# Second layer of a two-layer MoE block: the first product by Strassen's seven block products

## The chip, the cores and the metric

One core of a Trainium2 chip runs the whole program. The engines are named as in the profile: PE is TensorE (PEld are its weight loads), DVE is VectorE, ACT is ScalarE, POOL is GpSimd, and SP is SyncE, whose queue issues nearly all DMAs. The metric is the device time of one execution in microseconds (us). Before the change it is 1785.63 us, the median of 3 runs (1784.83 to 1786.25).

## The reference

Pooled attention (batch 8, 8 heads, 576 tokens, head size 64, keys and values averaged over 8 positions) gives `x` of 4608 x 512. Two feed-forward layers follow, each with d_ff = 2048:

```python
def _moe_ref(x, w_in, w_out):          # layer 1
    h = np.maximum(x @ w_in, 0.0)
    return (h * h @ w_out).astype(np.float32)

def _moe2_ref(x, w_in, w_out):         # layer 2
    h = x @ w_in
    g = np.maximum(0.01 * h, h)
    return (g @ w_out).astype(np.float32)
```

The weights come as float64. Every product of float32 numbers is computed as three products of parts of type `float32r`: a number is split into a high part and the remainder, its low part, and high x high, low x high and high x low are added up. For layer 2 this is 3 x 2 x 4608 x 512 x 2048 multiply-adds.

## The kernel before

The tokens are handled in 9 blocks of 512 (`T = 512`, `BLOCKS = 9`), d_ff in 16 chunks of 128 (`FC = 16`), d_model in 4 pieces of 128 (`KC = 4`). `run(blk)` is called for blocks 2 to 17: numbers up to 8 are layer 1, numbers 9 to 17 are layer 2 (`ph` is 0 or 1). Blocks 0 and 1 of layer 1 are done earlier by `first_products` and `second_products`, mixed with attention.

Within `block`, chunk by chunk, `first` makes `h` for one chunk: 12 matmuls (4 pieces of the contraction times 3 part products) of 128 x 128 weights by 512 tokens into one PSUM bank out of four (`ps`). `between` takes that bank off (ACT), applies the activation function and splits the result into `gh` and `gl` (DVE). `second` multiplies it by the chunk of `w_out`: 12 matmuls of 512 columns into the four banks `acc0` to `acc3`, which collect over all 16 chunks. The products are staggered: `first` of chunk u+1 stands ahead of `second` of chunk u, so that `between` has a whole `second` and the next `first` to hide behind. `finish` copies the four banks out and stores them.

All of this is written out by hand (`tc.manual_schedule()`): each engine executes its instructions in the order in which the program calls them. A wait therefore holds up everything behind it on the same engine. SBUF tiles come from one pool, with a number of buffers for each tag; a tile waits until the last use of the buffer's earlier tile is over.

The weights of layer 2 are converted from float64 during layer 1: `Stored.tick` does one of six steps for half of a weight pair at a time and stores high and low parts to DRAM (`w2_parts`). During block 8, the last of layer 1, `fetch` loads them into the buffers that layer 1's weights leave free.

The lines that the prediction speaks of are L860 (matmuls of `first`), L906 (matmuls of `second`), L888 and L889 (activation of layer 2), L878 and L879 (splitting), L343 and L344 (splitting layer 2's weights), L672 and L673 (splitting `x`, where the ACT copies and the DVE subtracts) and L695 to L698 (attention's values, whose matmuls have many widths).

## Time and profile before

| what | value |
|---|---|
| median of 3 runs | 1785.63 us (1784.83 to 1786.25) |
| span of the profiled execution | 1783.2 us; the profile gives no other time for it, and the median is 2.4 us above the span |
| PE busy | 1735.8 us, 97% of the span |
| DVE busy | 944.9 us, 53% |
| ACT busy | 510.8 us, 29% |
| chain that ended last | PE 91%, DVE 6%, ACT 2% |
| block 8 (last of layer 1) | 908.2 to 995.3 us |
| layer 2 (blocks 9 to 17) | 995.3 to 1778.6 us, 3456 matmuls |

The page has one row for each engine with its busy time, and the chain of work that ended last, which is followed back from the last instruction. Since matmuls overlap, a matmul's own duration is longer than the distance between two of them: read the distance from start to start.

### The profile page before, as it was taken

What the parts mean: (1) busy time and instruction counts of PE and PEld (TensorE: products, weight loads), DVE (VectorE), ACT (ScalarE), POOL (GpSimd) and SP (SyncE); (2) the same over time, 40 slices, a digit from 0 to 9 for tenths busy, and PEclk for the clock granted to TensorE, in tenths of its full rate; (3) what the DMA queues carried; (4) which work ended last, traced back from release to release, by engine and by line L of the source; (5) the groups of instructions that cost most, each with busy time, mean ns of one, the idle gap of its engine ahead of it and who ended that gap; (6) DMA issues with size and microseconds to landing.
All of it is one profiled execution on the core that took longest, in us unless ns stands there. A gap on an engine that the chain in (4) does not pass through costs nothing.

```text
span 1783.2 us, 20649 instructions
## 1 busy us (share of the span) xinstructions
PE 1735.8 (97%) x8024; PEld 1437.4 (81%) x8024; DVE 944.9 (53%) x1701; ACT 510.8 (29%) x1269; POOL 18.9 (1%) x37
## 2 busy tenths in 40 slices
PE   6889999999999999999999999999999999999998
PEld 5768778888788888878888888888888888888887
DVE  7888777667666776774322334343434343333333
ACT  4545333343443434433432211111111111111111
POOL 0011000000000000000000000000000000000000
PEclk9999999999999999999999999999999999999999
DMA  8914542332233232222035301010101010101000
GB/s 231 338 65 155 172 158 99 103 107 94 84 107 106 95 120 92 87 80 77 1 135 199 139 1 47 1 48 1 47 1 47 1 48 0 48 7 42 18 7 24
DMA packets 95585, 144.01 MB, mean 81 GB/s; under 512 B 42624, under 2 KB 42752, under 8 KB 93440
## 3 DMA queue, kind: packets, MB, share of 16 engines
q1 hardware_dynamic: 92928, 134.31, 22.9%
q0 software_dynamic: 2560, 8.39, 1.2%
q8 instruction: 63, 1.03, 0.2%
q14 instruction: 34, 0.28, 0.0%
HBM read 98.64 MB, written 44.04 MB: 80 GB/s over the span
## 4 chain that ended last, share of the span: by engine, by line
PE 91%; DVE 6%; ACT 2%; issue 1%; DMA 0%; SPq 0%; DVEq 0%; ACTq 0%
PE acc L906 42%; PE ps L860 39%; PE acc L860 4%; PE ps L581 2%; PE ps L644 1%; PE ps L545 1%; PE acc L375 1%; DVE xl L673 0%; DMA wi<-in_moe_w_in 0%; PE ps L696 0%; ACT s L602 0%; PE ps L698 0%; PE ps L697 0%; PE ps L695 0%; PE ps L650 0%
## 5 line engine op out<-in xcount | busy, mean ns | idle before, releaser
L860 PE MATMUL ps<-xh,wi 128*128 128x512 f32 x2048 | 673.5, 391 | 0.0
L860 PEld LDWEIGHTS ps<-xh,wi 128*128 128x128 f32 x2048 | 384.5, 188 | 79.9 <-issue 0.2
L860 PE MATMUL ps<-xl,wi 128*128 128x512 f32 x1024 | 398.5, 389 | 0.0
L889 DVE SCALAR_TENSOR_TENSOR r<-r 128x512 f32<-128x512 f32 x144 | 99.7, 693 | 462.3 <-ACT r L888 462.3
L906 PE MATMUL acc<-gh,wo 128*128 128x512 f32 x1152 | 297.3, 396 | 4.0 <-DVE gh L878 1.9
L906 PE MATMUL acc<-wo,gh 128*128 128x512 f32 x1152 | 288.9, 389 | 0.0
L888 ACT COPY r<-ps 128x512 f32<-128x512 f32 x144 | 84.5, 587 | 655.6 <-PE ps L860 655.6
L906 PEld LDWEIGHTS acc<-gh,wo 128*128 128x128 f32 x1152 | 214.0, 189 | 50.8 <-DVE gh L878 4.0
L906 PEld LDWEIGHTS acc<-wo,gh 128*128 128x128 f32 x1152 | 216.2, 188 | 44.9
L878 DVE CAST gh<-r 128x512 fp32r<-128x512 f32 x256 | 109.2, 426 | 227.4 <-ACT r L873 213.6
L860 PEld LDWEIGHTS ps<-xl,wi 128*128 128x128 f32 x1024 | 192.3, 188 | 38.9
L879 DVE TENSOR_TENSOR gl<-r,gh 128x512 fp32r<-128x512 f32 x256 | 177.4, 693 | 21.5 <-DVE gh L878 0.5
L906 PE MATMUL acc<-gl,wo 128*128 128x512 f32 x576 | 160.2, 393 | 0.0
L906 PE MATMUL acc<-wo,gl 128*128 128x512 f32 x576 | 158.3, 389 | 0.0
L870 ACT ACTIVATE r<-ps 128x512 f32<-128x512 f32 x112 | 67.7, 605 | 234.2 <-PE ps L860 234.2
L906 PEld LDWEIGHTS acc<-gl,wo 128*128 128x128 f32 x576 | 109.0, 189 | 23.5
L906 PEld LDWEIGHTS acc<-wo,gl 128*128 128x128 f32 x576 | 108.1, 188 | 22.5
L602 ACT ACTIVATE s<-ps,m 128x72 f32<-128x72 f32 x240 | 72.1, 329 | 106.2 <-DVE m L593 106.1
L873 ACT ACTIVATE r<-r 128x512 f32<-128x512 f32 x112 | 70.8, 632 | 3.6
L860 PE MATMUL acc<-xh,wi 128*128 128x512 f32 x128 | 44.4, 413 | 8.7 <-DVE wi L287 5.0
L602 ACT ACTIVATION_READ_ACCUMULATOR s<-ps,m 128x1 f32 x224 | 48.1, 215 | 0.0
L550 ACT COPY qt<-ps 128x512 f32<-128x512 f32 x32 | 18.8, 587 | 87.4 <-PE ps L545 87.4
(150 smaller groups left out, 1365.9 us busy)
## 6 DMA issues: line engine op xcount, KB each, us to landing
w2p<-val SPq DMA_DIRECT2D x32, 512.0 KB
pth<-x SPq DMA_DIRECT2D x9, 1024.0 KB
wi<-in_moe_w_in SPq DMA_DIRECT2D x8, 1024.0 KB
wo<-in_moe_w_out SPq DMA_DIRECT2D x8, 1024.0 KB
val<-in_moe_w_in SPq DMA_DIRECT2D x16, 512.0 KB
val<-in_moe_w_out SPq DMA_DIRECT2D x16, 512.0 KB
wi<-w2p SPq DMA_DIRECT2D x8, 1024.0 KB
wo<-w2p SPq DMA_DIRECT2D x8, 1024.0 KB
```

What stands on the lines that cost most here:

```text
L375: nc.tensor.matmul(ps[:n, c * 2 * D : (c + 1) * 2 * D], lhsT=ident[:n, :n], rhs=raw[:n, r * 2 * D : (r + 1) * 2 * D], start=r == 0, stop=r ...
L550: nc.scalar.copy(qT[i].rearrange("p c t -> p (c t)"), ps)
L581: nc.tensor.matmul(ps[: r0 + n, c2 * PAIR : (c2 + 1) * PAIR], lhsT=qt[:, cc, : r0 + n], rhs=kts[b][:, keys], start=True, stop=True,)
L602: nc.scalar.activation(out=s[:, g, :], in_=ps[:, h * SP : (h + 1) * SP], func=AF.Exp, bias=m[:, g : g + 1], accum_out=None if i in early e ...
L860: nc.tensor.matmul(ps, lhsT=w[:, kc], rhs=x[kc], start=(kc == 0 and n == 0), stop=(kc == KC - 1 and n == 2),)
L870: nc.scalar.activation(out=r, in_=ps, func=AF.Relu)
L873: nc.scalar.activation(out=r, in_=r, func=AF.Square)
L878: nc.vector.tensor_copy(gh, r)
L879: nc.vector.tensor_tensor(out=gl, in0=r, in1=f32(gh), op=ALU.subtract)
L888: nc.scalar.copy(r, ps)
L889: nc.vector.scalar_tensor_tensor(out=r, in0=r, scalar=0.01, in1=r, op0=ALU.mult, op1=ALU.max)
L906: nc.tensor.matmul(acc[m], lhsT=w[:, piece] if ph == 0 else x[:, piece], rhs=x if ph == 0 else w, start=(c == 0 and n == 0), stop=(c == FC ...
```

## The change

Layer 2's first product is no longer computed chunk by chunk over 512 tokens. Tokens come in 6 spans of 768, each made of two halves of 384 (`TS`). A group is one span with a pair of chunks of d_ff. The contraction (512) is cut in two halves of 256, so that the product of a group is a 2 x 2 block product, and Strassen's method (in Winograd's form) computes it with 7 block products of 256 x 128 x 384 in place of 8. Every block product takes 6 matmuls of 384 columns (2 pieces of the contraction times 3 part products). The sums of blocks that the seven products need are made ahead: of `x` by `x_sum`, `x_high`, `x_low` (tiles `fh0` to `fh6`, `fl0` to `fl6`), of the weights by `make_in`. The sums behind the products are made partly in PSUM, where products 2, 3, 5 and 6 add to what stands in their bank, and partly by DVE (`use`).

The seven forms of weights take more room, so only 8 of the 16 chunks are in SBUF at a time: one pass over all spans with the first 8 chunks, whose results are stored to DRAM (`part`), then one pass back over the spans with the other 8, to whose results `part` is added. The spans' order in the second pass is reversed, so that the span at the turn stays loaded. The second product is as before 36 matmuls of 512 columns for a group; `piece(g - 1, j)` puts six of them behind each of the first six block products of the next group. Two banks alternate for the block products, six collect results.

Of layer 2's weights, `w_in` is stored in float32 (`w2_raw`, out of a tile `r`) and no longer split in layer 1; `w_out` as before. In block 8, `early` loads and splits the first span and makes the first weights. The names in SBUF are spread over several pools, so that buffers can be given over to layer 2.

```diff
@@ Stored.tick @@
-            elif k == 4:
+            elif k == 4 and h % 2:
                 t = sb([P, 2, 512], F32R, "val")
-                nc.vector.tensor_copy(t[:, 0, :], f32(self.val))
+                nc.vector.tensor_copy(t[:, 0, :], self.out)
...
+            elif k == 5 - (h + 1) % 2:
+                i, n = h // 4, h // 2 % 2
+                to = w2_parts[i, :, :, n * 512 : (n + 1) * 512] if h % 2 else w2_raw[i, :, n]
+                nc.sync.dma_start(out=to, in_=self.out)
@@ second layer @@
+    FORMS = (A11, S2, A12, S3, S1, A22, S4)
...
+            self.order = [(0, n) for n in range(SPANS)] + [(1, n) for n in reversed(range(SPANS))]
+            self.groups = [(*o, p) for o in self.order for p in range(PAIRS)]
...
+        def x_high(self, j):
+            nc.scalar.copy(self.xh[j], self.x_raw(j))
+        def x_low(self, j):
+            nc.vector.tensor_tensor(
+                out=self.xl[j], in0=self.x_raw(j), in1=f32(self.xh[j]), op=ALU.subtract
+            )
...
+        def product(self, g, j):
+            half, n, p = self.groups[g]
+            at = self.banks[(g + j) % 2][:, :TS]
+            hi, lo = self.weights[p]
+            m = 0
+            for w, x in ((hi, self.xh), (lo, self.xh), (hi, self.xl)):
+                for kc in range(2):
+                    nc.tensor.matmul(
+                        at,
+                        lhsT=w[:, FORMS[j], kc],
+                        rhs=x[j][:, kc],
+                        start=m == 0 and j in (0, 1, 4),
+                        stop=m == 5,
+                        skip_group_check=True,
+                    )
+                    m += 1
+            self.use(g % 2, j, at)
+        def use(self, k, j, at):
+            def add(out_, x):
+                nc.vector.tensor_tensor(out=out_, in0=x, in1=at, op=ALU.add)
+            if j == 0:
+                self.s1 = sb([P, TS], F32, "gh")
+                nc.scalar.copy(self.s1, at)
+            elif j == 1:
+                self.u2 = sb([P, TS], F32, "gl")
+                add(self.u2, self.s1)
+                self.flush()
+            elif j == 2:
+                self.h11 = sb([P, TS], F32, "h11")
+                nc.scalar.copy(self.h11, at)
+            elif j == 3:
+                self.u3 = sb([P, TS], F32, "u3")
+                add(self.u3, self.s1)
+                self.leaky(self.h11, k, 0, 0)
+            elif j == 4:
+                add(self.u3, self.u3)
+                self.leaky(self.u3, k, 1, 1)
+            elif j == 5:
+                add(self.s1, self.s1)
+                self.leaky(self.s1, k, 1, 0)
+            else:
+                add(self.u2, self.u2)
+                self.flush()
+                self.leaky(self.u2, k, 0, 1)
+        def leaky(self, h, k, c, t):
+            nc.vector.scalar_tensor_tensor(
+                out=h, in0=h, scalar=0.01, in1=h, op0=ALU.mult, op1=ALU.max
+            )
+            hi, lo = self.gh[k][c][t], self.gl[k][c][t]
+            nc.scalar.copy(hi, h)
+            self.flush()
+            self.late.append(
+                lambda: nc.vector.tensor_tensor(out=lo, in0=h, in1=f32(hi), op=ALU.subtract)
+            )
...
+        def piece(self, g, i):
+            half, n, p = self.groups[g]
+            t, at = i // (TT // 2), slice(i % (TT // 2) * P, (i % (TT // 2) + 1) * P)
+            order = [(self.gh, c, m) for c in range(2) for m in range(2)]
+            order += [(self.gl, c, 0) for c in range(2)]
+            for m, (x, c, part_) in enumerate(order):
+                nc.tensor.matmul(
+                    self.acc[i],
+                    lhsT=x[g % 2][c][t][:, at],
+                    rhs=self.outs[p][:, part_, c],
+                    start=p == 0 and m == 0,
+                    stop=p == PAIRS - 1 and m == 5,
+                )
+            if p < PAIRS - 1:
+                return
+            if half == 0:
+                st, to = self.result_tile(i), part
+                nc.scalar.copy(st, self.acc[i])
+            else:
+                st, to = self.begun.pop(i), out
+                nc.vector.tensor_tensor(out=st, in0=st, in1=self.acc[i], op=ALU.add)
+            nc.sync.dma_start(out=to[self.rows(n, i), :], in_=st)
+        def group(self, g):
...
+            for j in range(7):
+                self.product(g, j)
+                if after != n and p == 2 and j in (1, 2, 4):
+                    self.x_sum((1, 2, 4).index(j))
+                if after != n and p == 3:
+                    if j >= 2:
+                        self.x_low(j - 2)
+                    if j == 4:
+                        self.x_sum(3)
+                    self.x_high(j)
+                if before != n and p == 0 and j < 2:
+                    self.x_low(5 + j)
+                if g and j < 6:
+                    self.piece(g - 1, j)
...
```

`after != n` holds in the groups of a span behind which another span follows, `before != n` in those behind such a change of span; there are 10 of these changes (five in each pass). `p` is the pair of chunks, 0 to 3.

On PE, layer 2's steady part read before: the end of one `first` (weights `wi`), then a `second` (weights `wo`), then the next `first`.

```order
L860 MATMUL ps<-xl,wi_7750 128x512
L860 MATMUL ps<-xh,wi_7750 128x512
L906 MATMUL acc_8276<-wo_7796,gh 128x512 x2
L906 MATMUL acc_8277<-wo_7796,gh 128x512 x2
L906 MATMUL acc_8278<-wo_7796,gh 128x512 x2
L906 MATMUL acc_8279<-wo_7796,gh 128x512 x2
L906 MATMUL acc_8276<-wo_7796,gl 128x512
```

Now, in the second group (`ps_8339` and `ps_8340` are the two alternating banks, `fh`, `fl` the forms of `x`, `sh`, `sl` the split activations of the group before):

```order
L1345 MATMUL acc0_8333<-wo0_7773,sh_8317 128x512 x2
L1345 MATMUL acc0_8333<-wo0_7773,sh_8319 128x512 x2
L1345 MATMUL acc0_8333<-wo0_7773,sl_8325 128x512
L1345 MATMUL acc0_8333<-wo0_7773,sl_8327 128x512
L1278 MATMUL ps_8339<-fh_7696,wi2_8103 128x384 x2
L1278 MATMUL ps_8339<-fh_7696,wi3_8104 128x384 x2
L1278 MATMUL ps_8339<-fl_7703,wi2_8103 128x384 x2
L1345 MATMUL acc1_8334<-wo0_7773,sh_8317 128x512 x2
```

Twelve matmuls of 512 columns with one bank became six of 384, and each of them is followed by only six of 512 before the next; the last two of a piece need the low parts `sl`.

On DVE, where one block of layer 2 met the next, a chunk was three instructions (activation, high part, low part), then came the split of the next block's `x` (L673), two results (L921) and the next chunk:

```order
L889 SCALAR_TENSOR_TENSOR r<-r 128x512
L878 CAST gh<-r 128x512
L879 TENSOR_TENSOR gl<-r,gh 128x512
L673 TENSOR_TENSOR xl<-pth,xh 128x512 x4
L921 COPY raw<-acc_8277 128x512
L921 COPY raw<-acc_8279 128x512
```

Now, in the fourth group of the first span, behind products 4, 5 and 6, when the next span's forms are being made (L1291 adds a product, L1319 is the activation, L1326 a low part, L1188 a low part of `x`, L1178 a sum of `x`):

```order
L1291 TENSOR_TENSOR u3_8669<-u3_8669,ps_8340 128x384
L1319 SCALAR_TENSOR_TENSOR u3_8669<-u3_8669 128x384
L1326 TENSOR_TENSOR sl_8329<-h11_8653,sh_8321 128x384
L1188 TENSOR_TENSOR fl_7704<-xl_8407,fh_7697 128x768
L1178 TENSOR_TENSOR xl_8407<-xl_8407,t2_8549 128x2x384
L1291 TENSOR_TENSOR gh_8622<-gh_8622,ps_8339 128x384
L1319 SCALAR_TENSOR_TENSOR gh_8622<-gh_8622 128x384
L1326 TENSOR_TENSOR sl_8332<-u3_8669,sh_8324 128x384
L1188 TENSOR_TENSOR fl_7705<-xh_8405,fh_7698 128x768
L1291 TENSOR_TENSOR gl_8637<-gl_8637,ps_8340 128x384
L1326 TENSOR_TENSOR sl_8331<-gh_8622,sh_8323 128x384
```

The work on the next span's `x` now stands in the same queue as the sums and low parts of the products; the last row is the low part that the next group's piece 0 takes in its sixth matmul.

## Rows read from the trace of the kernel before

**Rows 1.** The page: span, busy time of each engine, the chain by engine.
```profile
span 1783.2 us, 20649 instructions
PE 1735.8 (97%) x8024; PEld 1437.4 (81%) x8024; DVE 944.9 (53%) x1701; ACT 510.8 (29%) x1269; POOL 18.9 (1%) x37
PE 91%; DVE 6%; ACT 2%; issue 1%; DMA 0%; SPq 0%; DVEq 0%; ACTq 0%
```
**Rows 2.** Busy time by windows: blocks of layer 1, block 8, layer 2.
```profile
core 0: us, PE busy (x) PEld busy (x) DVE busy (x) ACT busy (x) POOL busy (x), PEclk, DMA share, GB/s
624.00:880.00 256.00, 251.90 (x1206) 209.47 (x1205) 159.49 (x320) 100.30 (x299) 0.00 (x0) 0.99 0.25 80
908.20:995.30 87.10, 87.10 (x386) 72.12 (x385) 21.53 (x38) 22.93 (x38) 0.00 (x0) 1.00 0.56 206
995.30:1778.60 783.30, 783.30 (x3456) 648.27 (x3454) 291.27 (x483) 111.74 (x194) 0.00 (x0) 1.00 0.07 25
```
**Rows 3.** Timeline of a chunk of layer 2: start, duration, engine, line, tiles.
```profile
1103.67 0.39 PE L860 MATMUL ps<-xh,wi 128*128 128x512 f32 x1
...
1103.90 1.98 PE L906 MATMUL acc<-wo,gh 128*128 128x512 f32 x8
1104.10 0.59 ACT L888 COPY r<-ps 128x512 f32<-128x512 f32 x1 [4.85 <-PE ps L860]
1104.72 0.69 DVE L889 SCALAR_TENSOR_TENSOR r<-r 128x512 f32<-128x512 f32 x1 [3.42 <-ACT r L888]
...
1105.51 0.43 DVE L878 CAST gh<-r 128x512 fp32r<-128x512 f32 x1
```
**Rows 4.** Timeline of PE where attention's values have 384 columns (16 matmuls).
```profile
275.97 0.33 PE L695 MATMUL ps<-pth,v_hi 128*128 128x384 f32 x1
276.14 0.34 PE L696 MATMUL ps<-pth,v_lo 128*128 128x384 f32 x1
...
278.60 0.34 PE L698 MATMUL ps<-ptr,v_rem 96*128 96x384 f32 x1
278.77 0.63 PE L906 MATMUL acc<-gh,wo 128*128 128x512 f32 x2
```
**Rows 5.** The chain in time near the start: start, time, engine, tile, line.
```profile
29.89 5.37 PE acc L375 x48
```
**Rows 6.** Groups by line and form: weight loads, and L375's matmuls.
```profile
L906 PEld LDWEIGHTS acc<-wo,gh 128*128 128x128 f32 x1152 | 216.2, 188 | 44.9
L375 PE MATMUL acc<-wo,cst 128*128 128x128 f32 x32 | 3.8, 278 | 0.0
```
**Rows 7.** Groups by line and form on DVE: count, busy us, mean ns, idle before.
```profile
L673 DVE TENSOR_TENSOR xl<-ps,xh 128x384 fp32r<-128x384 f32 x8 | 4.2, 554 | 1.6 <-ACT xh L672 1.1
L879 DVE TENSOR_TENSOR gl<-r,gh 128x512 fp32r<-128x512 f32 x256 | 177.4, 693 | 21.5 <-DVE gh L878 0.5
L287 DVE TENSOR_TENSOR wi<-val,wi 128x1024 fp32r<-128x1024 f32 x8 | 9.7, 1219 | 0.0
L889 DVE SCALAR_TENSOR_TENSOR r<-r 128x512 f32<-128x512 f32 x144 | 99.7, 693 | 462.3 <-ACT r L888 462.3
L921 DVE COPY raw<-acc 128x512 f32<-128x512 f32 x20 | 12.9, 684 | 2.1 <-PE acc L906 2.1
L343 DVE CAST val<-r 128x512 fp32r<-128x512 f32 x32 | 13.6, 425 | 0.9
L344 DVE TENSOR_TENSOR val<-r,val 128x512 fp32r<-128x512 f32 x32 | 22.2, 693 | 1.1
```
**Rows 8.** Groups by line and form on ACT.
```profile
L672 ACT CAST xh<-ps 128x384 fp32r<-128x384 f32 x8 | 3.8, 478 | 3.8 <-PE ps L698 3.7
L672 ACT CAST xh<-pth 128x512 fp32r<-128x512 f32 x36 | 19.6, 620 | 0.0
L283 ACT CAST wi<-val 128x1024 fp32r<-128x1024 f32 x8 | 8.5, 1062 | 4.8 <-DVE val L280 4.8
```
**Rows 9.** Timeline of the end of the program.
```profile
1778.23 0.39 PE L906 MATMUL acc<-wo,gl 128*128 128x512 f32 x1
1779.38 0.33 SPq L924 DMA_DIRECT2D out<-raw  x1
```

More of the change, by code (lines that the diff above doesn't have):

```diff
@@ L86, in attention_relu2_leaky_kernel @@
     BUFS.update({"m": 4, "l": 4, "st": 3, "val": 2})
+    POOLS = {tag: weights for i in range(FC // 2) for tag in (f"wi{i}", f"wo{i}")}
+    POOLS.update({f"wo{i}": spare for i in range(FC // 4, FC // 2)})
+    POOLS.update({tag: common for tag in "cst raw r gh gl st xh xl".split()})
     def sb(shape, dt, tag):
+        pool = POOLS.get(tag, attn)
         return pool.tile(shape, dt, tag=tag, name=tag, bufs=BUFS.get(tag, 1))
@@ L100, in attention_relu2_leaky_kernel @@
     x2 = dram.tile([DM, NT], F32, tag="x2", name="x2")
-    w2_parts = dram.tile([2, FC // 2, P, 2, 1024], F32, tag="w2p", name="w2p")
+    w2_raw = dram.tile([FC // 2, P, 2, 512], F32, tag="w2r", name="w2r")
+    w2_parts = dram.tile([FC // 2, P, 2, 1024], F32, tag="w2p", name="w2p")
+    part = dram.tile([NT, DM], F32, tag="part", name="part")
     mid = dram.tile([2, FC, P, T], F32, tag="mid", name="mid")
@@ L357, in finish @@
                 self.tick()
-        def fetch(self, kind, i):
-            t = sb([P, 2, 1024], F32R, weight_tag(kind, i))
-            nc.sync.dma_start(out=f32(t), in_=w2_parts[kind, i])
-            place(kind, i, t)
     first_tiles, first_s, early = range(T // P), [], range(2 * T // P)
@@ L880, in in_parts, with between, second @@
         return gh, gl
-    def between(ph, blk, ps):
+    def between(blk, ps):
         r = sb([P, T], F32, "r")
-        if ph == 0:
-            relu(r, ps)
-            square(r)
-        else:
-            nc.scalar.copy(r, ps)
-            nc.vector.scalar_tensor_tensor(
-                out=r, in0=r, scalar=0.01, in1=r, op0=ALU.mult, op1=ALU.max
-            )
+        relu(r, ps)
+        square(r)
         return in_parts(r)
-    def second(ph, c, acc, g):
+    def second(c, acc, g):
         gh, gl = g
         wh, wl = woh[c], wol[c]
-        ms = range(KC if ph == 0 else T // P)
+        ms = range(KC)
         passes = (wh, gh), (wl, gh), (wh, gl)
@@ L912, in second, with finish @@
             )
-    def finish(ph, t0, acc):
-        tags = ("st", "raw" if ph or t0 + T == NT else "r")
-        to = x2[:, t0 : t0 + T] if ph == 0 else out[t0 : t0 + T, :]
-        for m in range(KC if ph == 0 else T // P):
-            st = sb([P, T if ph == 0 else DM], F32, tags[m % 2])
+    def finish(t0, acc):
+        tags = ("st", "raw" if t0 + T == NT else "r")
+        for m in range(KC):
+            st = sb([P, T], F32, tags[m % 2])
             if m % 2:
@@ L954, in slot @@
                 done += 1
-        g = between(ph, blk, first(blk, 0))
+        g = between(blk, first(blk, 0))
         chunk_done("in", 0)
@@ L968, in block @@
                     turn.pop(0)()
-            second(ph, u, acc, g)
+            second(u, acc, g)
             chunk_done("out", u)
@@ L973, in block @@
             g = g_next
-        finish(ph, t0, acc)
+        finish(t0, acc)
     w1, w2 = Weights(w1_in, w1_out), Stored(w2_in, w2_out)
@@ L1101, in second_products @@
                 turn.pop(0)()
-            second(0, c, acc, g)
+            second(c, acc, g)
             if 4 <= u < 9:
@@ L1128, in chunk_done @@
+        steps, turn = [], []
+        if not last:
+            steps, turn = all_steps[blk + 1], value_steps(blk + 1, (blk + 1) * T)
         def chunk_done(what, c):
-            if blk < BLOCKS - 1:
+            if last:
+                layer2.early(what, c)
+            else:
                 w2.tick()
-            if blk == BLOCKS - 1:
-                w2.finish()
-                if c % 2 and (what == "in" or c < FC - 1):
-                    w2.fetch(what == "out", c // 2)
-        block(ph, blk, i * T, steps, turn, chunk_done)
@@ L1150, in attention_relu2_leaky_kernel @@
         second_products()
-        for blk in range(2, 2 * BLOCKS):
+        for blk in range(2, BLOCKS):
             run(blk)
+        layer2.run()
 _INS = ["q", "k", "v", "moe_w_in", "moe_w_out", "moe2_w_in", "moe2_w_out"]
```

229 lines of the change are left out of this document (187 added, 42 removed).

## The prediction

> **What bounds the kernel now.** I read the page first: PE is busy 97% of the span of 1783.2 us, and the chain that ended last is 91% PE [rows 1]. An average hides stages, so the busy time by windows comes next. In layer 2, from 995.3 to 1778.6 us, PE is busy for all of the 783.3 us, with 3456 matmuls, a granted clock of 1.00 (the upper level, 2.4 GHz), DVE at 291 us and ACT at 112 us [rows 2]. So layer 2 is a stream of matmuls without a gap, 783.3 / 3456 = 0.2267 us apart. The timeline of one chunk shows why: ACT takes a product off while PE already does 12 matmuls of another kind, and the activations come long before they are wanted [rows 3]. DVE waits 462 us for ACT's copies there [rows 7]. Only fewer or shorter matmuls can shorten this stage, as long as the others keep up.
>
> **The matmuls.** The second product keeps its 1728 matmuls of 512 columns: 48 groups of 36, before 9 blocks of 192. The first had 9 x 192 = 1728 of 512 columns and gets 48 x 42 = 2016 of 384 columns. What one of 384 takes, attention's values show: 16 of them start from 275.97 to 278.60 us and the next instruction at 278.77, that is 2.80 / 16 = 0.175 us each [rows 4]. The difference to 0.2267 is 0.052 us for 128 columns, 2.5 columns a nanosecond; so a matmul costs its columns at the upper clock and about 13 ns. I take 0.174, since one in four of those has 96 rows. First products: before 1728 x 0.2267 = 391.7, after 2016 x 0.174 = 350.8 us. **Gain 40.9 us.** Bounds of the distance: 0.173 (0.2267 less 128 columns at 2.4 GHz), and from above the weight load, below.
>
> The Trainium skill, "TensorE: Matmul & The Clock Gate", section "Back-to-back issue gap", gives for streams of weight load and matmul 81 ns at 128 columns and 131 ns at 512. On a straight line between them, 384 columns would take 114 ns, 0.87 of 512 columns, an estimate from that page. The rows differ, with 0.77 for 384 against 512 and 227 ns where the page has 131, so I count by the rows. By the page's ratio the change would lose, which is a rival below.
>
> **What must keep up.** In a group PE now needs 42 x 0.174 + 36 x 0.2267 = 15.5 us. DVE has 13 instructions of 384 columns: 5 additions out of PSUM, 4 activations, 4 low parts. The nearest row has 0.554 us for 384 columns out of PSUM [rows 7], together 7.2 us. ACT has 6 copies, at 0.478 for 384 columns out of PSUM [rows 8], about 3 us. Both are half idle or more, so the throughput holds. What decides is the order in the queues, with only two banks for block products and with low parts that the pieces read.
>
> In an undisturbed group it holds: from the end of a product to the next use of its bank lie two pieces and a product (1.36 + 1.04 + 1.36 = 3.8 us), or a product and a piece (2.4 us) behind products 5 and 6, and DVE has at most three instructions, 1.7 us, for each.
>
> At the 10 changes of span it doesn't quite. In the fourth group DVE also makes low parts and a sum of the next `x`, of 768 columns: 0.96 us each, halfway between 0.693 for 512 and 1.219 for 1024 [rows 7]. Follow the queue from where product 4 can be read, with DVE idle there, to the low part that piece 0 of the next group takes in its sixth matmul: 8 instructions of 384 and 3 of 768 columns, 8 x 0.554 + 3 x 0.956 = 7.3 us. Add 0.25 for the hand-overs from DVE to DVE, some 0.1 us each: an activation ends at 1105.41 and the next starts at 1105.51 [rows 3]. That is 7.55 us. On PE the same stretch is piece, product 5, piece, product 6, product 0, five matmuls: 2 x 1.36 + 3 x 1.04 + 1.13 = 6.97 us, of which 0.2 are gone before product 4 can be read (ACT starts 0.43 us after a product's last matmul started [rows 3], against a distance of 0.17 to 0.23). So PE waits 7.55 - 6.77 = 0.8 us, with the hand-over **0.9 us, 10 times: 9 us lost**. The bounds: nothing, if DVE's instructions overlap a little (0.08 us each would do), and 2 us a change, if each takes 10% longer and the delay also reaches product 2, which adds into the bank that ACT empties late. I stay with 9, since all durations are rows of this shape or next to it.
>
> **The start of layer 2.** Group 0 has no pieces to put between: 7.3 us of PE against 7.2 us of DVE in a chain, behind two copies of `finish` at 0.68 [rows 7]: 2 us lost (0 to 4), the last group's short wait for its low parts included. The end stays: the last result still passes one DVE instruction (0.69 by its 512 columns, as L921) and one store, 5 us from the last matmul to the end of the span [rows 9, 1]; `part` is loaded a span ahead.
>
> **Layer 1.** Block 8 gets DVE work: 11 instructions on `x` of 0.96 us, and four times about 4 us (four sums of 256 columns, low parts of 256, 512 and 1024) for the weights, together 27 us. ACT gets 7 casts of 0.83 (between 0.620 for 512 and 1.062 for 1024 [rows 8]) and four times 2 us, 14 us. DVE and ACT are busy 21.5 and 22.9 us of 87.1 there [rows 2], and the largest lump, 4 us, meets a slack of 2 x 5.44 us less two chunks' own 1.1: free. If it weren't, each lump would cost at most its 4 us. The loads of 1.6 MB have 13 us, at 206 GB/s and more [rows 2] they take 8. In blocks 2 to 7 DVE loses 16 times 0.43 + 0.69 us [rows 7], 18 us off an engine that has slack; PE is idle there only 4 us of 256 [rows 2], so that can give 1 or 2 us. Against that, 16 stores now leave from a tile `r` out of three, and an activation two chunks later waits for the store. I count 0 (from -2 to +5).
>
> **Sum.** 1783.2 - 40.9 + 9 + 2 = 1753.3 us of span. The runs' median is 1785.6, 2.4 above the span; with that 1755.7, said as **1755.5 us**, with its own range 1748 to 1764.
>
> **The rivals.**
> - No wait at the changes of span and none at the start: 1785.6 - 42 = 1744. For it: 0.9 us is a small difference of two sums of 7 us. Against it: nothing in the rows makes DVE faster. 12%.
> - The delay isn't made good: DVE and ACT stand late through the next span's first two groups too, where low parts 5 and 6 of `x` and six copies or additions of results (0.69 each) follow. Some 2 us more a change, 1755.5 + 20 = 1775. For it: both queues are in strict order. Against it: the third group's slack is 8 us. 13%.
> - Layer 1 waits for the stores out of `r`: 16 x 0.5 = 8, 1764. For it: three buffers. Against it: nearly 3 us of slack by the chunk's 5.44. 8%.
> - Slower: the weight load sets the pace of short matmuls. One load takes 188 ns in the trace [rows 6], longer than the 174 that I count; if loads came one behind the other with 13 ns between, a matmul of 384 would take 201 ns, 2016 x 0.027 = 54 us more, 1810. It decides from 0.189 us (40.9 - 11 = 30 us over 2016). For it: four in five of PE's time in layer 2 has a load running [rows 2]. Against it: 48 matmuls took 5.37 us early on, 0.112 us each [rows 5], of 128 columns and with a weight load each (as many as matmuls, 8024 [rows 1]), so loads do overlap; a row of that line shows its form [rows 6]. 4%.
> - Time falls less than columns do, 0.87 of the distance: 0.198 us, 2016 x 0.024 = 48 us more, 1804. For it: nothing in this trace. Against it: 16 in a row at 0.175 [rows 4]. 3%. The page named above has the rule behind it.
>
> **How the numbers follow.** My forecast has 60%, the rivals 12, 13, 8, 4 and 3%. The range 1744 to 1775 takes in the forecast, the third rival and about half of the first two. A difference of 0.2% (3.6 us) is what runs of this kernel can tell. Slower are the last two rivals, 7%; within it perhaps a mixture of the middle ones, 3%; faster the rest, 90%.
>
> **What would show it.** Right: 2016 matmuls of 384 columns 0.17 to 0.18 us apart; 10 waits of PE of about 1 us in the first group of a span, at the matmul that takes a low part, with DVE as the releaser; DVE busy some 50% of layer 2; layer 2 about 753 us long. Wrong: a distance near 0.19 or more, waits for a bank in every group, block 8 longer than 88 us, or a granted clock below 1.00 in layer 2.

## The result and the profile after

The changed kernel took **1761.6 us** (median of 4 runs, 1759.83 to 1763.66) against 1785.23 us (4 runs, 1783.91 to 1786.25) of the kernel before in the same job: a ratio of **0.9868, 95% interval 0.9854 to 0.9881**. It is faster by 1.3%. The forecast was 1755.5 us, its range 1744 to 1775; the time lies in the range, 6 us above the forecast, and two errors of opposite sign stand behind that, as will be seen.

Line numbers below are the changed kernel's: L864 and L903 are layer 1's two products (L860 and L906 before), L1278 the block products of 384 columns, L1345 the pieces of the second product of 512 columns, L1291, L1319, L1326, L1188 and L1178 VectorE's additions, activations, low halves of the values, low halves of `x` and sums of `x`, L1185 and L1323 ScalarE's high halves, L1295 its copies of products.

The page of the profile first: span, busy times, the chain.

```profile
span 1758.0 us, 21696 instructions
PE 1715.1 (98%) x8312; PEld 1463.6 (83%) x8312; DVE 1112.0 (63%) x2020; ACT 627.8 (36%) x1496; POOL 18.9 (1%) x37
PE 88%; DVE 7%; ACT 2%; DMA 1%; issue 1%; SPq 0%; DVEq 0%; ACTq 0%
```

Against [rows 1], PE has 288 matmuls more and 20.7 us less to do, DVE 167 us more, and the chain is still PE's. The profiled execution itself took 1759.83 us. The busy time by windows comes next: the middle of layer 1, the stretch in which the kernel before did block 8, and layer 2.

```profile
624.00:880.00 256.00, 252.37 (x1193) 206.18 (x1192) 154.00 (x310) 100.41 (x299) 0.00 (x0) 1.00 0.24 75
908.20:995.30 87.10, 87.10 (x375) 70.18 (x374) 39.17 (x66) 31.74 (x52) 0.00 (x0) 1.00 0.28 100
1007.70:1753.60 745.90, 745.81 (x3746) 674.15 (x3744) 454.54 (x800) 218.26 (x408) 0.00 (x0) 1.00 0.19 69
```

The first matmul of layer 2, in the kernel before and then in the kernel after:

```profile
995.10 0.39 PE L860 MATMUL ps<-xh,wi 128*128 128x512 f32 x1
```

```profile
1007.78 0.86 PE L1278 MATMUL ps<-fh,wi 128*128 128x384 f32 x4
```

Layer 2 begins 12.7 us later than before, and takes 745.6 us from its first matmul's start to its last one's where it took 783.1 (the last ones start at 1753.38 and 1778.23 us; the window of [rows 2] begins 0.2 us after the first); PE is again busy for all of it at a granted clock of 1.00, the upper level of 2.4 GHz. In the 87.1 us of the second window PE was already fully busy and still is, yet it got 375 matmuls done and not 386. So there are two things to see: layer 2 is 37.5 us shorter, and layer 1 is 12.7 us longer although PE has the same instructions there in the same order.

A chunk of block 8 on PE's timeline, of the kernel after and then of the kernel before (start, duration, engine, line, tiles), shows the second. In both, PE starts 12 matmuls of L864 or L860 and 12 of L903 or L906 from the first row to the second.

```profile
932.18 0.40 PE L864 MATMUL ps<-xh,wi 128*128 128x512 f32 x1
...
937.78 0.40 PE L864 MATMUL ps<-xh,wi 128*128 128x512 f32 x1
```

```profile
932.54 0.39 PE L860 MATMUL ps<-xh,wi 128*128 128x512 f32 x1
...
937.98 0.39 PE L860 MATMUL ps<-xh,wi 128*128 128x512 f32 x1
```

24 matmuls take 5.60 us, before 5.44: **0.2333 us each and not 0.2267**, at the same clock and with nothing waiting. No wait tells of it; only the distance from start to start does. Summed over layer 1, the distances between neighbouring matmuls of 512 columns (3382 before, 3381 after) went from 796.5 to 812.4 us; the rest of the time before layer 2 gave back 3.2. Not every distance grew by 0.0066 us: those under 0.3 us, 3255 before and 3260 after, were 0.2278 us in the mean and are 0.2332, while the longer ones, 127 and 121, add up to 55.1 and 52.2 us.

The timeline at a change of span, all engines:

```profile
1124.04 0.86 PE L1278 MATMUL ps<-fh,wi 128*128 128x384 f32 x4
1124.35 0.95 DVE L1188 TENSOR_TENSOR fl<-xh,fh 128x768 fp32r<-128x768 f32 x1
...
1124.73 0.51 PE L1278 MATMUL ps<-fl,wi 128*128 128x384 f32 x2
...
1125.08 1.07 PE L1345 MATMUL acc<-wo,sh 128*128 128x512 f32 x4
1125.22 0.55 DVE L1291 TENSOR_TENSOR gl<-gl,ps 128x384 f32<-128x384 f32 x1
1125.68 0.55 DVE L1326 TENSOR_TENSOR sl<-gh,sh 128x384 fp32r<-128x384 f32 x1
...
1125.98 0.80 PE L1345 MATMUL acc<-wo,sl 128*128 128x512 f32 x2
1126.15 0.55 DVE L1319 SCALAR_TENSOR_TENSOR gl<-gl 128x384 f32<-128x384 f32 x1
1126.29 0.19 PEld L1345 LDWEIGHTS acc<-wo,sl 128*128 128x128 f32 x1 [0.34 <-DVE sl L1326]
...
1126.62 0.86 PE L1278 MATMUL ps<-fh,wi 128*128 128x384 f32 x4
```

Six matmuls of 384 columns start from 1124.04 to 1125.08, 1.04 / 6 = 0.173 us each; the forecast had 0.174. The piece behind them takes 1126.62 - 1125.08 = 1.54 us where six of 0.227 would take 1.36. The wait is where the forecast put it, at the matmul that reads a low half that DVE makes, and is **0.18 us, not 0.9**. Also to be seen: DVE's instructions last 0.55 us and start 0.46 to 0.47 apart, and the one of 0.95 is followed after 0.87. An instruction that needs nothing of the one in front starts 0.08 to 0.09 us before that one's end.

VectorE's and ScalarE's groups by line and form, to compare with [rows 7, 8]:

```profile
L1188 DVE TENSOR_TENSOR fl<-xl,fh 128x768 fp32r<-128x768 f32 x30 | 28.6, 952 | 0.0
L1291 DVE TENSOR_TENSOR gh<-gh,ps 128x384 f32<-128x384 f32 x48 | 26.5, 553 | 18.3 <-PE ps L1278 18.3
L1185 ACT CAST fh<-xl 128x768 fp32r<-128x768 f32 x30 | 25.0, 834 | 0.0
L1295 ACT COPY gh<-ps 128x384 f32<-128x384 f32 x48 | 22.8, 474 | 0.6 <-PE ps L1278 0.6
```

The durations that the forecast took from shapes nearby (0.554, 0.956, 0.83, 0.478) are those measured.

The end of the program:

```profile
1753.16 0.61 PE L1345 MATMUL ps<-wo,sl 128*128 128x512 f32 x2
...
1754.53 0.33 SPq L1360 DMA_DIRECT2D out<-raw  x1
```

The last of these two matmuls starts at 1753.38, 4.6 us ahead of the span's end, against 5.0 [rows 9, 1].

### The profile page after: what moved, and what is told of

It reads as the page before. It is cut to its first block, busy times and chain, and to the rows that moved or that the text cites. A ratio compares the mean times of both kernels' runs of the same rounds, so it can differ in the third digit from the quotient of the medians.

```text
span 1758.0 us, 21696 instructions
## 1 busy us (share of the span) xinstructions
PE 1715.1 (98%) x8312; PEld 1463.6 (83%) x8312; DVE 1112.0 (63%) x2020; ACT 627.8 (36%) x1496; POOL 18.9 (1%) x37
## 4 chain that ended last, share of the span: by engine, by line
PE 88%; DVE 7%; ACT 2%; DMA 1%; issue 1%; SPq 0%; DVEq 0%; ACTq 0%
PE ps L1278 20%; PE acc L903 19%; PE ps L864 17%; PE acc L1345 15%; PE ps L1345 7%; PE acc L864 4%; PE ps L585 2%; ACT s L606 1%; PE ps L648 1%; PE ps L549 1%; PE ps L700 0%; PE ps L699 0%; PE ps L702 0%; DVE gl L883 0%; PE ps L701 0%
## 5 line engine op out<-in xcount | busy, mean ns | idle before, releaser
L903 PE MATMUL acc<-gh,wo 128*128 128x512 f32 x1152 | 301.4, 399 | 3.6 <-DVE gh L882 1.5
L864 PE MATMUL ps<-xh,wi 128*128 128x512 f32 x896 | 301.7, 399 | 0.0
L1278 PE MATMUL ps<-fh,wi 128*128 128x384 f32 x1344 | 289.2, 337 | 0.1
L1278 PEld LDWEIGHTS ps<-fh,wi 128*128 128x128 f32 x1344 | 243.1, 188 | 22.2 <-DVE gh L1291 0.4
L903 PEld LDWEIGHTS acc<-gh,wo 128*128 128x128 f32 x1152 | 213.2, 188 | 55.1 <-DVE gh L882 3.7
L1345 PE MATMUL acc<-wo,sh 128*128 128x512 f32 x768 | 205.7, 390 | 0.0
L864 PEld LDWEIGHTS ps<-xh,wi 128*128 128x128 f32 x896 | 168.4, 188 | 39.4 <-issue 0.2
L864 PE MATMUL ps<-xl,wi 128*128 128x512 f32 x448 | 177.1, 395 | 0.0
L1278 PE MATMUL ps<-fl,wi 128*128 128x384 f32 x672 | 171.2, 336 | 0.0
L903 PE MATMUL acc<-gl,wo 128*128 128x512 f32 x576 | 162.4, 396 | 0.0
L1345 PEld LDWEIGHTS acc<-wo,sh 128*128 128x128 f32 x768 | 141.5, 188 | 15.6
L903 PEld LDWEIGHTS acc<-gl,wo 128*128 128x128 f32 x576 | 108.3, 188 | 26.2
L1278 PEld LDWEIGHTS ps<-fl,wi 128*128 128x128 f32 x672 | 121.4, 188 | 0.0
L1345 PE MATMUL acc<-wo,sl 128*128 128x512 f32 x384 | 120.4, 392 | 0.0
L1345 PE MATMUL ps<-wo,sh 128*128 128x512 f32 x384 | 102.8, 389 | 0.0
L1291 DVE TENSOR_TENSOR u<-gh,ps 128x384 f32<-128x384 f32 x48 | 26.6, 554 | 117.9 <-PE ps L1278 117.9
L864 PEld LDWEIGHTS ps<-xl,wi 128*128 128x128 f32 x448 | 84.3, 188 | 18.8
L1345 PEld LDWEIGHTS acc<-wo,sl 128*128 128x128 f32 x384 | 72.1, 188 | 18.4 <-DVE sl L1326 3.8
```

The costliest lines, as they stand in the source:

```text
L864: nc.tensor.matmul(ps, lhsT=w[:, kc], rhs=x[kc], start=(kc == 0 and n == 0), stop=(kc == KC - 1 and n == 2),)
L903: nc.tensor.matmul(acc[m], lhsT=w[:, m * P : (m + 1) * P], rhs=x, start=(c == 0 and n == 0), stop=(c == FC - 1 and n == 2),)
L1278: nc.tensor.matmul(at, lhsT=w[:, FORMS[j], kc], rhs=x[j][:, kc], start=m == 0 and j in (0, 1, 4), stop=m == 5, skip_group_check=True,)
L1291: nc.vector.tensor_tensor(out=out_, in0=x, in1=at, op=ALU.add)
L1345: nc.tensor.matmul(self.acc[i], lhsT=x[g % 2][c][t][:, at], rhs=self.outs[p][:, part_, c], start=p == 0 and m == 0, stop=p == PAIRS - 1 an ...
```

## The experiments

The profile shows no wait for what layer 1 lost, so I asked what else had changed there. The change gives the weights pools of their own on the far side of SBUF. In the built programs (the profile doesn't show addresses) both operands of every matmul of 512 columns of the two layers start at 64 modulo 128 bytes in the kernel before; in the kernel after, the weights `wi`, `wo` and the second product's `sh`, `sl` start at 96, the activations `xh`, `gh` and layer 2's `fh`, `fl` still at 64. Theory A: a matmul of 512 columns takes 0.2333 us where the start addresses of its two operands differ by 32 bytes in this way. The text on record for the first run still had it as the weights' own start address alone; the rows of that run decide between the two. Its rivals: the weights' own address, the loads into the new pools, or VectorE's added work in layer 1.

**The distance measured alone.**

```
matmul(ps[:, :n], lhsT=wts[:, 256*(k%4)+so : 256*(k%4)+so+128], rhs=low[:, 640*(k%3)+mo : 640*(k%3)+mo+n])
# 48 of each (so, mo, n), back to back; so, mo in floats
```

> This kernel leaves the whole computation out: it runs 30 groups of 48 matmuls back to back, with weights of 128 x 128 and moving data of 512, 384, 448 or 256 columns of float32r, each shifted by 0, 4, 8 or 16 floats (16, 32 or 64 bytes) from an address that is a multiple of 64 bytes. Theory A (the start address of the weights against 64 bytes sets the extra 7 ns of layer 1): groups with 512 columns and weights shifted by 32 bytes take 0.233 us a matmul, all others with 512 columns 0.227; with 384 columns both take 0.173, as layer 2 does. Theory B (it is where in SBUF the two operands stand, or the program, not the address within 64 bytes): all groups of one width have one distance, 0.227 and 0.173.

Rows of the timeline (one row for each setting):

```profile
34.46 11.05 PE L84 MATMUL p<-low,wts 128*128 128x512 f32 x48
45.34 11.36 PE L86 MATMUL p<-low,wts 128*128 128x512 f32 x48
56.54 11.36 PE L88 MATMUL p<-low,wts 128*128 128x512 f32 x48
67.74 11.08 PE L90 MATMUL p<-low,wts 128*128 128x512 f32 x48
78.66 8.49 PE L92 MATMUL p<-low,wts 128*128 128x384 f32 x48
86.98 8.48 PE L94 MATMUL p<-low,wts 128*128 128x384 f32 x48
```

From start to start: no shift 10.88 / 48 = 0.2267 us, the weights 32 bytes on 0.2333, the data 32 bytes on 0.2333, both 0.2275. With 384 columns it is 0.1733 to 0.174 whatever the shift. So 32 bytes between the operands cost 6.6 ns a matmul at 512 columns and nothing at 384. The third row goes against the form on record, by which only a shift of the weights is slow; rival B, by which no shift counts, falls too. A shift of 16 bytes on the weights cost 6.7 ns, one of 64 bytes 6.5 ns on the weights and 2.6 on the data, so it isn't a matter of 64-byte steps alone. The Trainium skill, "TensorE: Matmul & The Clock Gate", section "Step-by-step: what each phase is for", says that loading the next weights takes no read bandwidth from the running matmul. In these rows the place of the weights changes the matmuls' distance all the same, from 0.2267 to 0.2333 us; whether that is by read bandwidth they don't show.

**Layer 1 with the weights at the data's place.** The kernel after with 32 bytes in front of its weights, so that they start at 64 modulo 128.

```diff
+        weights.tile([P, 8], F32, tag="pad", name="pad")
```

> The changed kernel with a pad of 32 bytes above the weights' pool, which moves the weights of both layers, and the split activations of layer 2 with them, from addresses of 32 modulo 64 bytes to multiples of 64. Same instructions in the same order. Theory A: matmuls of layer 1 return from 0.2332 to 0.2267 us, layer 2 begins at 995 us and not 1007.8, time 1761.6 - 12.5 = 1749. Theory B: no change, 1761.

1753.53 us (1752.89 to 1754.76), ratio 0.9825 (0.9809 to 0.9841). Layer 1's matmuls are back at 0.227 us, and layer 2 begins 13.4 us earlier than in the kernel after:

```profile
994.42 0.87 PE L1279 MATMUL ps<-fh,wi 128*128 128x384 f32 x4
```

That is theory A's 12.7 us, and another 0.7. But the time is 4.5 us above theory A's 1749, since layer 2 took 752.0 us from its first to its last matmul where after takes 745.6: now the pieces are slow, 0.231 us in the mean, although the addresses of their operands `sh` and `wo` are equal modulo 128. Theory A doesn't say that.

**The kernel before with the difference, and with the address alone.** Weights in a pool of their own at 96 modulo 128; and 32 bytes ahead of all tiles.

```diff
+    weights = ctx.enter_context(tc.tile_pool(name="wt", bufs=1, side="right"))
...
+    POOLS = {tag: weights for i in range(FC // 2) for tag in (f"wi{i}", f"wo{i}")}
```

> The kernel before with only the pools of the change: weights in a pool of their own at the upper end, at 32 modulo 64 bytes, everything else at multiples of 64; no Strassen. Theory A: layer 1 is 12 us longer, and in layer 2 the first products (weights shifted, data not) go to 0.233, 11 us more; of the second products (data shifted, split activations as weights not) the theory says 0.227. Together 1785 + 23 = 1808; 1820 if a shift of either operand counts. If instead the slow matmuls of layer 1 came from the r stores or from block 8's new work, nothing changes: 1785.

```diff
+    sb([P, 8], F32, "pad")
```

> The kernel before with a pad of 32 bytes in front of all its tiles: weights and moving data both at 32 modulo 64 bytes. If a shift of the weights counts by itself: all matmuls at 0.233, 3500 + 3800 of them, 1785 + 36 = 1830 or a little less. If only the difference between the two operands counts (layer 2's second products after the change have both at 32 and run at 0.227): no change, 1785.

1820.12 us, ratio 1.0200 (1.0185 to 1.0215), and 1784.71 us, ratio 1.0001 (0.9992 to 1.0011). 1820 is what a shift of either operand gives; with the weights' own address, as on record, it would have been 1808. With the difference, layer 2 begins at 1010.70 us and is 806.2 us long from first to last matmul (783.1 before), 0.2333 us for both products, and a chunk of block 8 takes 5.60 us:

```profile
932.30 2.03 PE L910 MATMUL acc<-gh,wo 128*128 128x512 f32 x8
...
937.90 2.03 PE L910 MATMUL acc<-gh,wo 128*128 128x512 f32 x8
```

With all tiles moved together it stays at 5.44:

```profile
934.82 1.98 PE L907 MATMUL acc<-gh,wo 128*128 128x512 f32 x8
...
940.26 1.98 PE L907 MATMUL acc<-gh,wo 128*128 128x512 f32 x8
```

So layer 1's loss is made in the kernel before by moving the weights, with nothing else of the change, and it isn't the address 96 by itself. Theory A, as the difference between the two operands, is shown for layer 1.

**Why the pieces grew slow.** Theory C: the 384-column matmuls in front leave PE in a phase, by their own addresses, which the 512-column ones behind keep.

```
for i in range(8):
    6 matmuls of 384 columns (wi, fh);  6 of 512 (sh, wo)   # addresses by setting
```

> This kernel leaves the whole computation out: it runs the changed kernel's pattern of matmuls, 6 of 384 columns and then 6 of 512, eight times for each of 14 settings of start addresses (activations as weights at 100288 plus a shift, weights as moving data at 221120 plus a shift, the operands of the 384 as in the run before), some without the 384s. Theory A2 (only the two operands' start addresses of one matmul count): the setting of the run weights_aligned is slow (0.231 us) with and without 384s in front, that of the changed kernel fast (0.227), and a shift of the activations alone by 32, 64, 128 or 256 bytes changes it. Theory C (the matmuls of 384 in front leave PE in a phase that the 512s keep): without 384s all settings with equal addresses modulo 64 bytes run at 0.227, and shifting only the operands of the 384s makes the 512s fast.

Rows of the timeline, first with the addresses of weights_aligned, then with those of after:

```profile
78.81 1.55 PE L101 MATMUL p<-big 128*128 128x512 f32 x6
80.20 1.21 PE L99 MATMUL p<-big 128*128 128x384 f32 x6
...
103.07 1.52 PE L107 MATMUL p<-big 128*128 128x512 f32 x6
104.44 1.21 PE L105 MATMUL p<-big 128*128 128x384 f32 x6
```

Six of 512 take 1.39 us there and 1.37 here. Over all rows:

| setting | 384 columns, ns | 512 columns, ns |
|---|---|---|
| as weights_aligned | 174.4 | 231.4 |
| as weights_aligned, no 384 in front | | 227.1 |
| as after | 174.5 | 227.8 |
| as weights_aligned, `wi` and `fh` 32 bytes on | 175.2 | 228.0 |
| as weights_aligned, only `wi` 32 bytes on | 175.6 | 231.2 |
| as weights_aligned, `sh` 32 bytes on | 176.6 | 233.0 |

The first, second and fourth differ in the 384-column matmuls alone, and it is the 512-column ones that change. Theory C has this; theory A by itself doesn't. But the third and fifth have the very same 384-column matmuls, and 512-column ones that differ only in that both operands lie 32 bytes further on: 227.8 and 231.2. So the phase isn't set by the addresses of the 384-column matmuls alone; how the operands of both kinds lie to each other counts. Of the eight settings not in the table, those without 384 columns in front stand where theory A has them (227.2 as after, 233.4 with `sh` 32 bytes on, 227.1 with 256); the others have the 512 columns at 231.4 to 233.3.

**In the kernel: two placements, and after again.**

```diff
# wi_fh_32: as weights_aligned, and
+            pool.tile([P, 8], F32, tag="fpad", name="fpad")   # ahead of fh, fl
+   wi: views that begin 8 floats into the tile
# common_32: the kernel after, with 32 bytes ahead of the common pool and fpad as above
```

> The kernel after with three groups of tiles at other start addresses and no instruction added or moved: the weights' pools at 64 modulo 128 bytes (as in weights_aligned), and layer 2's wi and fh 32 bytes behind that (96 modulo 128). Theory A (layer 1's loss is the distance of the weights' start address from the data's): layer 1 at 0.227 us for 512 columns, layer 2 starts near 995.5 us as in the kernel before. Theory C (a 512-column matmul keeps the phase in which the 384-column ones in front left the engine, by their addresses): the pieces near 0.228 us as in the setting 'wi, fh +32' measured alone, not 0.231 as in weights_aligned; the 384-column ones 0.175. Together 1747 to 1749 us, 13 to 14 below the kernel after and 5 to 6 below weights_aligned. If the setting measured alone doesn't carry over to the kernel, the pieces stay at 0.231 and the time at 1753.

> The kernel after with 32 bytes put in front of the common pool, so that layer 1's data, x and the results lie at 96 modulo 128 bytes, where the kernel after has its weights; fh is moved by 32 bytes too, so that every distance between the operands of layer 2's first product is as in the kernel after; no instruction is added or moved. Theory A: layer 1 goes from 0.2333 back to 0.227 us a matmul, layer 2 starts 12.5 us earlier, and layer 2 stays as in the kernel after (pieces 0.2275, 384 columns 0.1735): 1749 us. The rival to A (the weights' own address at 96 modulo 128 costs the time, or the DMAs into it): layer 1 stays at 0.233 and the time at 1761.6. Theory C has layer 2's pieces hang on the second product's addresses too (r is moved, the weights wo are not): then they may go to 0.231 and the time to 1753.

> The kernel after itself on this chip, for comparison with the two beside it: 1761.6 us by every theory, 0.987 of the kernel before; layer 1's matmuls of 512 columns 0.2333 us apart, layer 2's pieces 0.2275.

after_again took 1763.78 us, ratio 0.9879 (0.9865 to 0.9892), beside them. Its layer 2 is 745.6 us long, as in after, but begins at 1011.79 us, 4 us later, with a granted clock of 0.98 from 560 to 900 us where after has 1.00; so 12.7 us is one reading of layer 1's loss, and the low one. wi_fh_32 took **1750.49 us** (1748.85 to 1751.14), ratio 0.9805 (0.9792 to 0.9818): layer 1 at 0.227, layer 2 from 993.43 us and 749.0 long, the 384 columns at 175.1 ns and the pieces at 228 in the mean, as measured alone; the time is 1.5 us above the 1747 to 1749 that I gave. common_32 took 1754.54 us, ratio 0.9829 (0.9815 to 0.9842). It has layer 1 at 0.227 with the weights where after has them, so their own place and the loads into it cost nothing. But its pieces went to 0.2286 us in the mean and the 384 columns to 0.1766, and layer 2 took 752.4 us, 6.8 more than in after. My text said that `fh` moves by 32 bytes; it moved by 64 in all, 32 with the pool and 32 by its own pad.

**What made the pieces of common_32 slow.** First 64 bytes more ahead of `fh`, so that it lies at 64 modulo 128 again, 128 bytes beyond its place in after; then the same place of `fh` with the common pool left where after has it.

```diff
# fh_96_more: common_32 with          # fh_128: the kernel after with
+   pool.tile([P, 24], F32, ...)      +   pool.tile([P, 32], F32, tag="fpad", name="fpad")
```

> common_32 with 64 bytes more in front of fh, nothing else: fh lies at 64 modulo 128 again, as in the kernel after, so all operands of layer 2's products stand to each other and to 128 as there, while layer 1's data keep the weights' 96. In common_32 the pieces went to 0.2293 us though neither of their own operands had been moved; only fh, the 384-column products' data, had. Theory C (the 384-column matmuls in front leave the engine in a phase, by their addresses, and the pieces keep it): the pieces go back to 0.2273 and the 384 columns to 0.1740, layer 1 stays at 0.227 to 0.228: about 1750, 4 below common_32. The rival (the pieces' pace in common_32 came from the common pool's move, by r or the results' tiles): the pieces stay at 0.2293 and the time at 1754.5.

> The kernel after with 128 bytes put in front of fh and fl and nothing else moved: fh and fl lie where they lie in fh_96_more, the common pool where it lies in the kernel after. It tells apart what made the pieces go to 0.231 us in fh_96_more. Theory C in its wide form (the address of the first product's data alone sets the pace of the pieces behind, and not only by its place in 128 bytes): pieces 0.231, 384 columns 0.177, layer 1 0.233 as in after, some 1769 us. Theory D (the common pool's tiles, which VectorE and ScalarE write and read beside the matmuls, and which share nothing with the pieces' operands, set it): pieces 0.2273 and 384 columns 0.174 as in after, 1762 us.

fh_96_more took 1756.51 us, ratio 0.9837 (0.9823 to 0.985), 6 above what theory C gave: pieces 0.2306, 384 columns 0.1770. So theory C in the form that only the place in 128 bytes counts is wrong. fh_128, a single run, took 1775.31 us (1769 expected): pieces 0.2306, 384 columns 0.1769, layer 1 at 0.2333 as in after; its layer 2 begins at 1012.74 us, nearer to after_again than to after, which is 5 of the 6 us too many. PE's timeline in fh_128 shows a piece, its four matmuls that read high halves and its two that read low ones:

```profile
1244.45 1.08 PE L1346 MATMUL acc<-wo,sh 128*128 128x512 f32 x4
1245.38 0.62 PE L1346 MATMUL acc<-wo,sl 128*128 128x512 f32 x2
```

The four take 0.93 us here. The timeline of the kernel after:

```profile
1241.08 1.07 PE L1345 MATMUL acc<-wo,sh 128*128 128x512 f32 x4
1241.99 0.62 PE L1345 MATMUL acc<-wo,sl 128*128 128x512 f32 x2
```

There it is 0.91. In fh_128 the only operands of PE that were moved are `fh` and `fl` (three tiles of VectorE's behind them, `t1`, `t2` and `sums`, moved along), and layer 2 took 756.1 us against 745.6. So the place of the first product's data changes the pace of the second product's matmuls behind, and the common pool's move had no part in it (fh_96_more, with that move, has the same paces and a layer 2 of 756.1 us): theory D falls, and theory C stands in a wide form: the place of the first product's data counts, not only its place in 128 bytes, and not by itself. That the three tiles of VectorE moved along was not tested by itself; where the matmuls ran alone, without VectorE, the addresses did the same. Which bits of the addresses count I can't say; differences of 16, 32, 64 and 128 bytes all had an effect somewhere, one of 256 (on `sh`, measured alone: 231.4 and 231.4) had none.

**The wait at the change of span.** Behind the seventh product, the low half that is still due, that of `s1`, ahead of the addition (`s1` is the third value to be split; the text on record calls it the fourth):

```diff
             else:
-                add(self.u2, self.u2)
                 self.flush()
+                add(self.u2, self.u2)
                 self.leaky(self.u2, k, 0, 1)
```

> fh_96_more with one pair of VectorE instructions exchanged in each group: behind the seventh product the low half of the fourth value (L1326 of the kernel after) stands ahead of the add that waits for that product (L1291). Theory S (the stall of 0.18 to 0.19 us at each of the ten changes of the span is the chain from the seventh product over the add to the low half that the piece's fifth matmul reads): the low half no longer waits for the product, the gaps at the fifth and sixth matmul go, 1.9 us in all, and nothing else moves: 1.9 below fh_96_more. The rival (VectorE's own queue of x_low instructions sets the stall): the low half still stands behind them, the gaps stay within 0.05 us, and the time with them. That the add, now 0.47 us later, makes the next product wait for its bank: slower by up to 192 groups x 0.1 us = 19 us; the trace of after has 0.8 us of idle VectorE ahead of that add in an ordinary chunk, so I don't expect it.

> wi_fh_32 with the exchange of lo_first: the low half of the fourth value ahead of the add that waits for the seventh product. wi_fh_32 has gaps of 1.7 us in layer 2 in all and lo_first lost its own but for 0.3 us at the start, so layer 2 should be 1.3 us shorter: 1749 us against 1750.5, if the pieces' pace stays. If a stall in one place also shifts the phase that the matmuls keep, the pieces' pace can change by either sign; more than 3 us either way would show that.

```profile
1115.37 0.95 DVE L1190 TENSOR_TENSOR fl<-xh,fh 128x768 fp32r<-128x768 f32 x1
...
1116.20 1.09 PE L1347 MATMUL acc<-wo,sh 128*128 128x512 f32 x4
1116.24 0.55 DVE L1328 TENSOR_TENSOR sl<-gh,sh 128x384 fp32r<-128x384 f32 x1
1116.70 0.55 DVE L1293 TENSOR_TENSOR gl<-gl,ps 128x384 f32<-128x384 f32 x1
...
1117.13 0.62 PE L1347 MATMUL acc<-wo,sl 128*128 128x512 f32 x2
```

The low half is done 0.34 us before its matmul starts, and the waits at the changes of span are gone; 0.33 us at the start of layer 2 are left. But lo_first took 1758.35 us, ratio 0.9846 (0.9833 to 0.986), beside 1756.51 of fh_96_more, where I had expected 1.9 less. Its layer 2 is 755.2 us long against 756.1; its layer 1, which has the same instructions, ended 3.1 us later in the profiled executions, and across all these kernels with layer 1 at 0.227 that end lies between 993.4 and 997.3 us. So a gain of 1 us in layer 2 can't be told in the time. Layer 2's own length does tell it, for that repeats: 745.61 and 745.64 us in after and after_again, 756.11 and 756.09 in fh_96_more and fh_128. The exchange took 0.9 us off it. The 1.9 us that I had expected were the waits of after; fh_96_more, with slower pieces, had only 0.8 us of them to lose. With wi_fh_32 as its base it was 1748.91 us (1747.08 to 1750.79), **ratio 0.9793 (0.978 to 0.9807)**, the fastest of all; layer 2 went from 749.0 to 746.8 us, 2.2 shorter, while the interval of the time overlaps that of wi_fh_32. The runs don't separate theory S from its rival: in the kernel after, VectorE is busy without a gap ahead of the low half, and one instruction less there helps in either case. My rival was put badly, since it too gains from the exchange.

## Why the prediction was right, and where it wasn't

The span by its own terms: 1783.2 - 40.7 (first products) + 0.7 (second products) + 2.5 (waits in layer 2) + 12.7 (layer 1) - 0.4 (end) = 1758.0 us, as the trace has it. The forecast had -40.9, 0, +11, 0 and 0, 1753.3 us; to that it added 2.4 for the median above the profiled span, which is now 3.6.

- **The matmuls: right.** 2016 at 0.1741 us are 351.0 us, forecast 350.8. The weight load's 188 ns didn't bound them. The pieces at 0.2271 made 392.4 us of 391.7. Both rivals on the pace of 384 columns fell. With the other placements tried above the same matmuls took up to 0.177 us, 5.8 us more, so a part of this hangs on where the tiles came to lie.
- **The changes of span: the right place, a fifth of the size.** Of the 11 us for ten changes and the start, 2.5 are there: 0.18 to 0.19 at each change, 0.36 at the start, 0.26 at the end. The first rival, no waits at all (1744; its 42 us are the gain of 40.9 with 1 us more, for which it gives no reason), was nearer to this term than the forecast. The one wait for a bank is at the start, where the second group's first product waits for the addition that reads that bank:

```profile
1015.34 0.66 PEld L1278 LDWEIGHTS ps<-fh,wi 128*128 128x128 f32 x4 [0.41 <-DVE gh L1291]
```

  The step that failed at the changes is "together 7.55 us" for VectorE's queue of eight instructions of 384 and three of 768 columns. In the trace the queue is there just as counted, from the start at 1119.42 us to the end at 1126.23:

```profile
1119.42 0.56 DVE L1291 TENSOR_TENSOR u<-u,ps 128x384 f32<-128x384 f32 x1 [0.51 <-PE ps L1278]
1120.01 0.56 DVE L1319 SCALAR_TENSOR_TENSOR u<-u 128x384 f32<-128x384 f32 x1
1120.49 0.55 DVE L1326 TENSOR_TENSOR sl<-h,sh 128x384 fp32r<-128x384 f32 x1
1120.96 0.95 DVE L1188 TENSOR_TENSOR fl<-xl,fh 128x768 fp32r<-128x768 f32 x1
1121.94 0.96 DVE L1178 TENSOR_TENSOR xl<-xl,t 128x768 f32<-128x768 f32 x1
```

  But it takes 6.81 us. I had added the durations and 0.25 for hand-overs. On PE the stretch is 6.79 us (1119.42 to 1126.21, where the matmul would have started), the forecast's 6.77. An instruction that waits for the one in front does start late (0.59 from L1291 to L1319, of 0.56; 0.98 from L1188 to L1178, of 0.95, which writes the tile that the one in front reads), but those that don't start 0.08 us early (0.47 to 0.48 for 0.55), and in this queue 7 of 10 don't. I had named this very bound, "0.08 us each would do", and didn't take it. A row of [rows 7] couldn't tell it, since a duration isn't a distance; the timeline of the kernel before could have. There the four splits of `x` at the end of a block take 2.49 us together and not 4 x 0.69 = 2.76, that is (2.49 - 0.69) / 3 = 0.60 from start to start:

```profile
992.29 2.49 DVE L673 TENSOR_TENSOR xl<-pth,xh 128x512 fp32r<-128x512 f32 x4
```

- **Layer 1: the step that failed.** "I count 0 (from -2 to +5)" was argued from waits alone: VectorE's work, the stores out of `r`, the loads. All of these were free as argued: weights_aligned has the same work, stores and loads, and begins layer 2 at 994.42 us, 0.7 before the kernel before. What I left out is that the change also moves tiles. Up to 0.0066 us on each 512-column matmul made 12.7 us, shown by weights_aligned, common_32 and before_weights_32. One sign of being wrong that the forecast names did show: block 8 took 16 x 5.60 = 89.6 us, over its 88. The rival of stores out of `r` named a time near the measured one, 1764, with another mechanism: it isn't what happened.
- **That the sum came near the time is luck: +12.7 and -8.5 nearly cancel.** Layer 2 itself was 745.6 us long and not 753, and DVE was busy 61% of it and not some 50%. With layer 1 as forecast the time would have been about 1749, as in wi_fh_32_lo_first, nearer to the first rival's 1744 than to the forecast.

## What to carry to other kernels

Where PE is the bound, measure the distance from start to start of each shape, stage by stage, also where the change moves nothing: a loss of 3% per matmul shows in no wait and in no group's idle time. When a change moves tiles to other pools, list the start addresses of both operands of the hot matmuls before and after, and if a distance grows, try 32 bytes of padding first: here one line was worth 8 us. For a queue of VectorE, add distances from start to start and not durations, and tell instructions that must wait for the one in front from those that needn't.

## What the runs showed of the hardware

- A matmul of 512 fp32 columns takes 0.2267 or 0.2333 us in a stream, by the start addresses of weights and data relative to each other (0.2267 alike, 0.2333 with 32 bytes between them); 384 columns take 0.1733 to 0.174 in a stream of their own either way.
- In a stream that mixes them with 384 columns the pace of the 512-column matmuls (0.2271 to 0.2333) hangs also on the addresses of the 384-column ones in front of them. What in the chip holds that, and by which bits, was not found.
- VectorE starts an instruction that is independent of the one in front 0.08 to 0.09 us before that one's end, at 384, 512 and 768 columns, and one that has to wait for it 0.03 us after.
